# Left keys of two exponential tiles turned in one transpose, in an attention and MoE kernel

## The chip, the cores and the metric

The kernel runs on one core of a Trainium2 chip. The metric is the device time of one execution in microseconds; three runs of the kernel before gave 951.61 (median), 950.59 and 954.29. The engines are called PE (matrix products and transposes), DVE (vector), ACT (scalar, exponentials), POOL (GpSimd) and SP (issues the DMAs).

## The reference

```python
q_rot, k_rot = rotate(q), rotate(k)          # q, k, v: 4 x 8 heads x 576 x 64, f32
scores = 1/sqrt(64) * q_rot @ k_rot.T        # 576 x 576 for each of 32 heads
attn = exp(scores - max(scores, -1)); attn = attn / (sum(attn, -1) + 1e-9)
x = (attn @ v) -> 2304 x 512                 # heads side by side
x = (1/(1+exp(-(x @ w_gate))) * (x @ w_val)) @ w_out          # weights given in float64
h = x @ w_in; solu = h * softmax(h)
out = (solu - mean) / sqrt(var + 1e-6) * g_ln @ w_out2
```

## The kernel before

**Three stages.** Attention takes the first 290 us or so of the trace, then come the gated products (stage B) and the last layer (stage C). The change touches attention alone. There, work goes by 16 pairs of heads. A pair has 9 tiles of scores: four tiles of 128 queries for each head, and between them one tile (n = 4, `order[n] is None`) with the 64 left-over queries of both heads. 576 keys are 512 main keys and 64 left keys.

**One tile, step by step.** `scores` (L372) multiplies a tile of queries with the 576 keys, in two halves of 288 columns, into PSUM (tile `s`, two buffers). `row_max` (L379, tile `nm`) reduces it on DVE. `exps` (L384, tile `e`) takes exponentials on ACT. `transpose_e` (L442, tile `te`) turns the four 128-key blocks of `e` on PE, into one of three PSUM buffers of the pool `ps_t`. Each turned tile is then written twice: ACT writes the high part (`evac_h`, L433), and DVE the low part, which is the PSUM value less that high part (`evac_l`, L436). `attend` (L483, tile `av`) multiplies the result with v.

**Left keys.** `transpose_left` (L463, tile `tk`) runs twice for each pair, once for each head. It turns the last 64 columns of each of the head's four `e` tiles (64 partitions out, 128 columns in), into one PSUM tile of 64 x 512. ACT writes the high part to partitions 0 to 63 of `etl`, DVE the low part to partitions 64 to 127. `transpose_corner` (L454, tile `tl`) does so for the tile of left queries.

**Blocks of k and q.** For each pair `qk_bank` (L303, L306, tile `tq`) turns rotated k and q in three parts; ACT and DVE write them as blocks `st0` and `st1` (lines L433 and L436 again). `stack` copies blocks by DMA (L317 to L323), so that partitions 64 to 127 get what the low parts need. The first pair has no time for that and copies with ACT and DVE (`stack_first`, L332 to L338).

**What sets the order.** It is written out: an agenda gives each step a slot (`SLOTS`), nine slots to a pair, and one loop emits a slot: row maximum of the tile, the ACT copies, the exponentials, the DVE subtractions, then the scores of the next tile and the steps of the agenda. Each engine works off its own rows in that order. `left=(6, 11)` places the two `transpose_left` of a pair: head 0 in slot 6 of the pair, head 1 in slot 2 of the next. Weights for stage B are decoded on the side (`val`, `mag`, `w`), some operations to a pair from the fifth pair on.

Of the kernel before, what the change touches and what calls it, by code (L numbers as in the profile page):

```python
# [8 lines left out]
F32 = mybir.dt.float32  # L9
F32R = mybir.dt.float32r  # L10
# [10 lines left out]
def kernel(  # L21
# [21 lines left out]
    nc = tc.nc  # L43
    B, H, S, D = q.shape
# [3 lines left out]
    P = 128  # L48
    MAIN, LEFT, HALF = 512, 64, 288
# [14 lines left out]
    ident = const.tile([P, P], F32, name="ident")  # L64
# [112 lines left out]
    enter = a_ctx.enter_context  # L177
# [2 lines left out]
    rawv_p = prep_ctx.enter_context(tc.tile_pool(name="rawv", bufs=2, side="right"))  # L180
    rot_p = prep_ctx.enter_context(tc.tile_pool(name="rot", bufs=1, side="right"))
    qk_p = enter(tc.tile_pool(name="qkT", bufs=2))
    wt_p = enter(tc.tile_pool(name="wt", bufs=2))
    rt_p = enter(tc.tile_pool(name="rt", bufs=1))
    uw_p = enter(tc.tile_pool(name="uw", bufs=4))
    st_p = enter(tc.tile_pool(name="st", bufs=4))
    et_p = enter(tc.tile_pool(name="et", bufs=1))
    vs_p = enter(tc.tile_pool(name="vs", bufs=2))
    e_p = enter(tc.tile_pool(name="e", bufs=7))
    dr_p = enter(tc.tile_pool(name="dr", bufs=2, space=bass.MemoryType.DRAM))  # L190
    ps_2 = ctx.enter_context(tc.tile_pool(name="ps_2", bufs=2, space=PSUM, side="right"))
    ps_t = enter(tc.tile_pool(name="ps_t", bufs=3, space=PSUM))
# [4 lines left out]
    raws, stacks, vraws, vss = {}, {}, {}, {}  # L197
# [92 lines left out]

    def qk_bank(i, part):

        raw = turned[i].rearrange("p i h d -> p i (h d)")
        if part == 0:
            stacks[i, 0] = qk_p.tile([P, 2, 2, S], F32R, tag="st0", name=f"st0_{i}")
            stacks[i, 1] = qk_p.tile([P, 3, S], F32R, tag="st1", name=f"st1_{i}")
        st = stacks[i, 0]
        ps = ps_t.tile([P, 512], F32, tag="t", name=f"tq{i}_{part}")  # L300
        if part < 2:
            for r in range(4):
                nc.tensor.transpose(ps[:, r * P:(r + 1) * P], raw[:, 4 * part + r, :], ident)  # L303
            h_out, l_out, src = st[:, 0, part, 0:MAIN], st[:, 1, part, 0:MAIN], ps
        else:
            nc.tensor.transpose(ps[:, 0:P], raw[:, 8, :], ident)  # L306
            h_out, l_out = st[:, 0, :, MAIN:S], st[:, 1, :, MAIN:S]
            src = ps[:, 0:P].rearrange("p (a t) -> p a t", a=2)
        return [(h_out, l_out, src)]

    def stack(i, step):

        s0, s1 = stacks[i, 0].bitcast(F32), stacks[i, 1].bitcast(F32)
        flat = s0.rearrange("p a b s -> p (a b) s")
        dma = nc.sync.dma_start
        if step == 0:
            dma(out=s1[D:P, 0:2], in_=flat[D:P, 0:2])  # L317
            dma(out=s1[0:D, 2], in_=flat[D:P, 0])
            dma(out=s1[0:D, 0:2], in_=flat[D:P, 2:4])
            dma(out=s1[D:P, 2], in_=flat[D:P, 2])  # L320
        else:
            dma(out=flat[D:P, 0:2], in_=flat[0:D, 2:4])
            dma(out=flat[D:P, 2], in_=flat[0:D, 0])  # L323

    def stack_first(h, step):

        near, far = slice(h * D, (h + 1) * D), slice((1 - h) * D, (2 - h) * D)
        if step < 2:
            c = slice(0, MAIN) if step == 0 else slice(MAIN, S)
            srcs = [(first[kq] if step == 0 else first[2][:, kq])[near] for kq in range(2)]  # L330
            for kq, ps in enumerate(srcs):
                nc.scalar.copy(out=st_block(0, h, kq)[near, c], in_=ps)  # L332
            for kq, ps in enumerate(srcs):
                hi = st_block(0, h, kq)[near, c].bitcast(F32)
                nc.vector.tensor_sub(out=st_block(0, h, kq)[far, c], in0=ps, in1=hi)
        else:
            nc.scalar.copy(out=st_block(0, h, 2)[far], in_=st_block(0, h, 0)[near].bitcast(F32))
            nc.vector.tensor_copy(st_block(0, h, 2)[near], st_block(0, h, 0)[far].bitcast(F32))  # L338

    first = []  # L340

# [2 lines left out]
            (nc.gpsimd, nc.vector)[SLOTS["left_eng"]].tensor_copy(qtl[i % 2][:, 3 * h, :], st_block(i, h, 1)[:, MAIN:S].bitcast(F32))  # L344

    def st_block(i, h, j):
        t = stacks[i, h]
        return t[:, j // 2, j % 2, :] if h == 0 else t[:, j, :]


    order = [(0, 0), (0, 1), (0, 2), (0, 3), None, (1, 0), (1, 1), (1, 2), (1, 3)]
    NTL = len(order)
    e_tiles = {}
    sums = {}
    wts = {}
# [74 lines left out]
    etl = et_p.tile([P, 2, S], F32R, name="etl")  # L430
# [101 lines left out]
    def at(g, kind, fn, *args):  # L532
# [155 lines left out]
    if True:  # L688
# [154 lines left out]
    for t, (s, bl, f) in enumerate(items):  # L843
# [17 lines left out]
        if f % FG in (1, 2) and t + FG < len(items):  # L861
            s2, bl2, _ = items[t + FG]
# [4 lines left out]
    enter = c_ctx.enter_context  # L867
# [256 lines left out]
```

## Time and profile before

| | |
|---|---|
| runs, median (lowest, highest) | 951.61 us (950.59, 954.29) |
| profiled execution | 953.07 us, its span 951.2 us |
| attention, first to last row maximum | 14.7 to 286.4 us |
| PE busy over the span | 97% |
| DVE, ACT, POOL busy over the span | 67%, 52%, 47% |

The shares over the span are means over stages that have little in common; attention has to be read by itself. A row of the timeline gives the start, the length, engine, line, operation, what is written and read, the count, and in brackets the idle time before it and what ended that; an idle time that is too short to be told has no bracket and is read from the starts and lengths. Instructions of one engine overlap a little, so that a start can lie before the end of the one ahead. PE's matrix products overlap far more: the distance of their starts tells the pace. A row of the windows gives from:to, the length, the busy time with the count of instructions for PE, PE's weight loads, DVE, ACT and POOL, then the granted clock of PE, the DMA share and GB/s.

### The profile page before, as it was taken

The page shows a single profiled execution, that of the slowest core. Times are in us where ns is not written, and L with a number is a line of the kernel's source. Part 1 is how long each engine was busy: PE and PEld are TensorE (multiplying, and loading weights), DVE is VectorE, ACT ScalarE, POOL GpSimd, SP SyncE. Part 2 cuts the span into 40 slices and gives each one's busy share as a digit, 9 for nine tenths or more (in the row PEclk, how much of TensorE's full clock was granted, in tenths as well). Part 3 has the DMA queues.
Part 4 walks back from the last instruction along what each step waited for, and adds up shares of the span by engine and source line. Part 5 has one row for each costly group of instructions (what it writes and reads, how often), then busy time and mean ns, then how long its engine had stood idle before and what let it go on. Part 6 is the DMA issues. An engine that isn't in the chain of part 4 may idle for free.

```text
span 951.2 us, 14449 instructions
## 1 busy us (share of the span) xinstructions
PE 922.0 (97%) x5128; PEld 798.2 (84%) x5128; DVE 641.1 (67%) x1069; ACT 498.7 (52%) x994; POOL 447.1 (47%) x356
## 2 busy tenths in 40 slices
PE   4999999999998999999999999999999989999998
PEld 3999999999997688887888898788898778888886
DVE  6999999999998943446164456345366896666661
ACT  5999999998995322223111223011123676666662
POOL 7678899898935532335232344314344431121110
PEclk9999999999999999999999999999999999999999
DMA  4668676776644211022001013101012243344332
GB/s 121 156 159 195 172 191 165 187 179 161 142 128 143 89 45 45 23 65 91 1 22 45 23 45 102 32 23 39 28 46 89 88 78 78 67 83 83 67 78 45
DMA packets 92233, 86.12 MB, mean 91 GB/s; under 512 B 51568, under 2 KB 76416, under 8 KB 92160
## 3 DMA queue, kind: packets, MB, share of 16 engines
q1 hardware_dynamic: 92160, 85.19, 35.2%
q8 instruction: 41, 0.67, 0.3%
q14 instruction: 32, 0.26, 0.1%
HBM read 46.83 MB, written 4.79 MB: 54 GB/s over the span
## 4 chain that ended last, share of the span: by engine, by line
PE 82%; DVE 9%; POOL 2%; issue 2%; ACT 2%; DMA 2%; SPq 0%; DVEq 0%; POOLq 0%; ACTq 0%
PE gv L682 9%; PE gv L683 9%; PE gv L681 9%; PE s L372 8%; PE av L483 7%; PE te L442 5%; PE y L791 4%; PE y L789 4%; PE y L790 4%; PE po L977 3%; PE po L979 3%; PE po L978 3%; PE ph L882 3%; PE ph L884 3%; PE ph L883 3%
## 5 line engine op out<-in xcount | busy, mean ns | idle before, releaser
L775 POOL TENSOR_TENSOR gs<-g,gs 128x512 fp32r<-128x512 f32 (+1 forms) x59 | 74.1, 1255 | 261.3 <-DVE gs L774 211.3
L770 ACT ACTIVATE sg<-gv 128x512 f32<-128x512 f32 (+1 forms) x60 | 33.3, 555 | 287.8 <-PE gv L683 287.8
L681 PE MATMUL gv<-xs,w 128*128 128x512 f32 (+1 forms) x480 | 176.8, 368 | 2.5 <-ACT w L137 2.5
L683 PE MATMUL gv<-xs,w 128*128 128x512 f32 (+1 forms) x480 | 176.9, 369 | 1.8 <-POOL w L138 1.7
L682 PE MATMUL gv<-xs,w 128*128 128x512 f32 (+1 forms) x480 | 176.9, 368 | 1.0 <-DVE xs L516 1.0
L772 DVE TENSOR_TENSOR g<-gv,sg 128x512 f32<-128x512 f32 (+1 forms) x60 | 38.2, 636 | 174.6 <-ACT sg L770 165.0
L384 ACT ACTIVATE e<-s,nm 128x576 f32<-128x576 f32 x144 | 107.3, 745 | 11.6 <-DVE nm L379 11.2
L379 DVE TENSOR_REDUCE nm<-s 128x1 f32<-128x576 f32 x144 | 107.2, 745 | 4.6 <-PE s L372 3.0
L683 PEld LDWEIGHTS gv<-xs,w 128*128 128x128 f32 x480 | 90.5, 189 | 18.2 <-POOL w L138 2.8
L436 DVE TENSOR_TENSOR et<-te,et 128x512 fp32r<-128x512 f32 x144 | 98.2, 684 | 10.6 <-ACT et L433 10.1
L372 PE MATMUL s<-st 128*128 128x288 f32 x512 | 100.2, 318 | 5.2 <-ACT e L384 2.6
L681 PEld LDWEIGHTS gv<-xs,w 128*128 128x128 f32 x480 | 90.1, 188 | 17.8 <-ACT w L137 3.3
L682 PEld LDWEIGHTS gv<-xs,w 128*128 128x128 f32 x480 | 90.1, 188 | 17.4 <-DVE xs L516 2.8
L483 PE MATMUL av<-et,vs 128*128 128x288 f32 x512 | 100.0, 316 | 0.5 <-DVE uw L634 0.3
L791 PE MATMUL y<-gs,w 128*128 128x512 f32 (+1 forms) x240 | 88.4, 368 | 0.1
L790 PE MATMUL y<-gs,w 128*128 128x512 f32 (+1 forms) x240 | 88.2, 368 | 0.0
L789 PE MATMUL y<-gs,w 128*128 128x512 f32 (+1 forms) x240 | 88.2, 367 | 0.0
L442 PE MATMUL te<-ident,e 128*128 128x128 f32 x576 | 86.0, 272 | 0.0
L433 ACT CAST et<-te 128x512 fp32r<-128x512 f32 x144 | 83.8, 584 | 3.0 <-PE te L442 2.9
L372 PEld LDWEIGHTS s<-st 128*128 128x128 f32 x512 | 74.6, 193 | 12.3 <-ACT e L384 7.6
L483 PEld LDWEIGHTS av<-et,vs 128*128 128x128 f32 x512 | 73.0, 189 | 4.2 <-DVE uw L634 2.5
L442 PEld LDWEIGHTS te<-ident,e 128*128 128x128 f32 x576 | 70.4, 140 | 0.2
(125 smaller groups left out, 1955.0 us busy)
## 6 DMA issues: line engine op xcount, KB each, us to landing
st<-st SPq DMA_DIRECT2D x45, 288.0 KB
wraw<-in_moe_w_out_dram SPq DMA_DIRECT2D x20, 512.0 KB
st<-st SPq DMA_DIRECT2D x45, 144.0 KB
wraw<-in_moe_w_gate_dram SPq DMA_DIRECT2D x12, 512.0 KB
wraw<-in_moe_w_val_dram SPq DMA_DIRECT2D x12, 512.0 KB
um<-uw SPq DMA_DIRECT2D x32, 144.0 KB
rawv<-in_v_dram SPq DMA_DIRECT2D x16, 256.0 KB
wraw<-in_moe_w_in_dram SPq DMA_DIRECT2D x8, 512.0 KB
```

What stands on the lines that cost most here:

```text
L372: nc.tensor.matmul(ps[:, j, :HALF], w, x, start=m == 0, stop=m == len(mm) - 1)
L379: nc.vector.tensor_reduce(out=nm, in_=ps[:, :, :HALF], axis=AX.XY, op=ALU.max, negate=True)
L384: nc.scalar.activation(out=e.rearrange("p (j c) -> p j c", j=2), in_=ps[:, :, :HALF], func=AF.Exp, bias=nm, accum_out=sums[i][:, n:n + 1],)
L436: nc.vector.tensor_sub(out=l_out, in0=ps, in1=h_out.bitcast(F32))
L442: nc.tensor.transpose(ps[:, r * P:(r + 1) * P], e[:, r * P:(r + 1) * P], ident)
L483: nc.tensor.matmul(av[:, :HALF], *mm[m], start=m == 0, stop=m == len(mm) - 1)
L681: nc.tensor.matmul(ps[:, :n], wh, x[:, 0, :n], start=kk == 0, stop=False)
L682: nc.tensor.matmul(ps[:, :n], wh, x[:, 1, :n], start=False, stop=False)
L683: nc.tensor.matmul(ps[:, :n], wl, x[:, 0, :n], start=False, stop=kk == KD - 1)
L789: nc.tensor.matmul(ys[m][:, :n], wh, g[:, 0, :n], start=first, stop=False)
L790: nc.tensor.matmul(ys[m][:, :n], wl, g[:, 0, :n], start=False, stop=False)
L791: nc.tensor.matmul(ys[m][:, :n], wh, g[:, 1, :n], start=False, stop=last)
```

## The change

Left keys come to stand at the other end in every second tile. For that the blocks of k are made 640 columns long, with the left keys at both ends, and odd tiles take their scores from column 0, even tiles from column 64. Two tiles of exponentials share one buffer of 1152 columns, so the left keys of an even tile and of the odd one behind it are neighbours, and one transpose turns both: two transposes of 128 x 128 in place of four of 64 x 128. The result has an upper half (even tiles) and a lower half (odd tiles) and is written by two ACT and two DVE instructions in place of one of each. `qk_bank` gets a further small transpose in its third part and writes 192 columns there in place of 128. The first pair's copies of blocks go to ACT (head 0) and to two DMAs (head 1). Buffers: `wt`, `um` from 2 to 1, `uw` from 4 to 3, `e` from 7 to four doubles and one single.

```diff
-    wt_p = enter(tc.tile_pool(name="wt", bufs=2))
+    wt_p = enter(tc.tile_pool(name="wt", bufs=1))
-    uw_p = enter(tc.tile_pool(name="uw", bufs=4))
+    uw_p = enter(tc.tile_pool(name="uw", bufs=3))
-    e_p = enter(tc.tile_pool(name="e", bufs=7))
+    e_p = enter(tc.tile_pool(name="e", bufs=4))
+    el_p = enter(tc.tile_pool(name="el", bufs=1))
...
+    KW = LEFT + S
+    K_AT, Q_AT, K2_AT = 0, KW, KW + S
+    BLOCKS = ((K_AT, KW), (Q_AT, S), (K2_AT, KW))
     def qk_bank(i, part):
...
-            nc.tensor.transpose(ps[:, 0:P], raw[:, 8, :], ident)
-            h_out, l_out = st[:, 0, :, MAIN:S], st[:, 1, :, MAIN:S]
-            src = ps[:, 0:P].rearrange("p (a t) -> p a t", a=2)
+            nc.tensor.transpose(ps[:, LEFT:LEFT + P], raw[:, 8, :], ident)
+            nc.tensor.transpose(ps[:, 0:LEFT], raw[0:LEFT, 8, :], ident[0:LEFT, 0:LEFT])
+            h_out, l_out = (x.rearrange("p (b t) -> p b t", t=LEFT)[:, 0:19:9] for x in (h, l))
+            src = ps[:, 0:3 * LEFT].rearrange("p (a t) -> p a t", a=3)
...
     def stack_first(h, step):
...
-            nc.scalar.copy(out=st_block(0, h, 2)[far], in_=st_block(0, h, 0)[near].bitcast(F32))
-            nc.vector.tensor_copy(st_block(0, h, 2)[near], st_block(0, h, 0)[far].bitcast(F32))
+            if h == 0:
+                nc.scalar.copy(out=st_block(0, h, 2)[far], in_=st_block(0, h, 0)[near].bitcast(F32))
+                nc.scalar.copy(out=st_block(0, h, 2)[near], in_=st_block(0, h, 0)[far].bitcast(F32))
+            else:
+                nc.sync.dma_start(out=st_block(0, h, 2)[far].bitcast(F32), in_=st_block(0, h, 0)[near].bitcast(F32))
+                nc.sync.dma_start(out=st_block(0, h, 2)[near].bitcast(F32), in_=st_block(0, h, 0)[far].bitcast(F32))
...
-            c = slice(j * HALF, (j + 1) * HALF)
+            k0 = j * HALF + (0 if order[n] is not None and order[n][1] % 2 else LEFT)
+            c = slice(k0, k0 + HALF)
...
     def transpose_left(i, h):
         ps = ps_t.tile([P, 512], F32, tag="t", name=f"tk{i}_{h}")
-        n0 = 5 * h
-        for qt in range(4):
-            nc.tensor.transpose(ps[0:LEFT, qt * P:(qt + 1) * P], e_tiles.pop((i, n0 + qt))[:, MAIN:S], ident)
-        return [(etl[0:LEFT, h, 0:MAIN], etl[LEFT:P, h, 0:MAIN], ps[0:LEFT, :])]
+        for m in range(2):
+            nc.tensor.transpose(ps[:, m * P:(m + 1) * P], e_both.pop((h, m))[:, MAIN:MAIN + P], ident)
+        x = etl[:, h, 0:MAIN].rearrange("p (m a t) -> p a m t", m=2, a=2)
+        src = ps[:, 0:2 * P].rearrange("p (m t) -> p m t", m=2)
+        up, down = slice(0, LEFT), slice(LEFT, P)
+        return [(x[up, 0], x[down, 0], src[up]), (x[down, 1], x[up, 1], src[down])]
...
-        first_b=(-1, -1, 2),
+        first_b=(-1, -1, 0),
```

**DVE around the second `transpose_left` of pair 10** (slots 1 to 4 of pair 11; a name's first number is the pair, then the tile). Before:

```order
L436 TENSOR_TENSOR st0_12_3189<-tq12_2_3284,st0_12_3189 128x2x64
L397 RECIPROCAL sum10_2925<-sum10_2925 128x9
L379 TENSOR_REDUCE nm11_3_3325<-s11_3_3300 128x1
L436 TENSOR_TENSOR et_245<-te10_8_3305,et_245 128x4x128
L436 TENSOR_TENSOR etl_131<-tk10_1_3314,etl_131 64x512
L379 TENSOR_REDUCE nm11_4_3364<-s11_4_3333 128x1
```

and in the changed kernel:

```order
L468 TENSOR_TENSOR st0_12_3161<-tq12_2_3254,st0_12_3161 128x3x64
L429 RECIPROCAL sum10_2899<-sum10_2899 128x9
L405 TENSOR_REDUCE nm11_3_3294<-s11_3_3271 128x1
L468 TENSOR_TENSOR et_251<-te10_8_3276,et_251 128x4x128
L468 TENSOR_TENSOR etl_134<-tk10_1_3285,etl_134 64x2x128 x2
L405 TENSOR_REDUCE nm11_4_3334<-s11_4_3303 128x1
```

One subtraction of 64 x 512 became two of 64 x 256 ahead of the row maximum of tile 4, and the one of `st0` is 192 columns wide in place of 128. The order is the same.

**PE at the same place.** Before:

```order
L306 MATMUL tq12_2_3284<-ident_70,turned12_3078 128x128
L372 MATMUL s11_3_3300<-st0_11_2905 128x288 x4
L442 MATMUL te10_8_3305<-ident_70,e10_8_3201 128x128 x4
L483 MATMUL av10_10_3310<-et_245,vs10_2940 128x288 x2
L463 MATMUL tk10_1_3314<-ident_70,e10_5_3115 64x128
L463 MATMUL tk10_1_3314<-ident_70,e10_6_3147 64x128
L463 MATMUL tk10_1_3314<-ident_70,e10_7_3175 64x128
L463 MATMUL tk10_1_3314<-ident_70,e10_8_3201 64x128
L372 MATMUL s11_4_3333<-st0_11_2905,qtl1_79 128x288 x2
```

and in the changed kernel:

```order
L315 MATMUL tq12_2_3254<-ident_70,turned12_3051 128x128
L316 MATMUL tq12_2_3254<-ident_70,turned12_3051 128x64
L398 MATMUL s11_3_3271<-st0_11_2880 128x288 x4
L475 MATMUL te10_8_3276<-ident_70,e10_7_3146 128x128 x4
L518 MATMUL av10_10_3281<-et_251,vs10_2914 128x288 x2
L495 MATMUL tk10_1_3285<-ident_70,e10_5_3088 128x128
L495 MATMUL tk10_1_3285<-ident_70,e10_7_3146 128x128
L398 MATMUL s11_4_3303<-st0_11_2880,qtl1_79 128x288 x2
```

Two of the four transposes of left keys are gone, and a transpose of 64 columns stands behind the third part of k and q.

## Rows read from the trace of the kernel before

**Rows 1.** The page: the chain of waits that ended last, by engine.

```profile
PE 82%; DVE 9%; POOL 2%; issue 2%; ACT 2%; DMA 2%; SPq 0%; DVEq 0%; POOLq 0%; ACTq 0%
```

**Rows 2.** Windows of attention, pairs 1 to 2 and 10 to 11.

```profile
199.39:210.24 10.85, 10.85 (x86) 10.27 (x86) 10.66 (x19) 10.34 (x26) 9.98 (x10) 1.00 0.69 180
210.24:216.49 6.25, 6.25 (x50) 5.91 (x49) 5.91 (x9) 5.13 (x13) 6.09 (x4) 1.00 0.68 154
...
46.15:57.00 10.85, 10.85 (x86) 10.31 (x86) 10.66 (x19) 10.35 (x26) 6.79 (x6) 1.00 0.54 143
57.00:62.85 5.85, 5.85 (x49) 5.72 (x48) 4.98 (x9) 5.00 (x12) 5.62 (x5) 1.00 0.85 189
```

**Rows 3.** Timeline of DVE from pair 10's turned tile 4 on.

```profile
199.39 0.69 DVE L436 TENSOR_TENSOR et<-te,et 128x512 fp32r<-128x512 f32 x1 [0.33 <-ACT et L433]
200.11 0.68 DVE L436 TENSOR_TENSOR etl<-tk,etl 64x512 fp32r<-64x512 f32 x1
200.83 0.76 DVE L379 TENSOR_REDUCE nm<-s 128x1 f32<-128x576 f32 x1
201.50 0.68 DVE L436 TENSOR_TENSOR et<-te,et 128x512 fp32r<-128x512 f32 x1
```

**Rows 4.** Timelines of ACT and DVE, pair 11, tile 4 to turned tile 4.

```profile
211.09 0.74 ACT L384 ACTIVATE e<-s,nm 128x576 f32<-128x576 f32 x1 [0.28 <-DVE nm L379]
...
216.49 0.69 DVE L436 TENSOR_TENSOR et<-te,et 128x512 fp32r<-128x512 f32 x1 [0.17 <-ACT et L433]
```

**Rows 5.** Groups by form, all of the span: busy us, mean ns.

```profile
L436 DVE TENSOR_TENSOR etl<-tk,etl 64x512 fp32r<-64x512 f32 x32 | 21.9, 683 | 1.0
...
L433 ACT CAST etl<-tk 64x512 fp32r<-64x512 f32 x32 | 18.6, 582 | 0.6
...
L436 DVE TENSOR_TENSOR etl<-tl,etl 64x128 fp32r<-64x128 f32 x16 | 4.5, 283 | 0.5
...
L433 ACT CAST etl<-tl 64x128 fp32r<-64x128 f32 x16 | 4.2, 260 | 0.1
```

**Rows 6.** Timelines of PE and ACT around pair 10's second left keys.

```profile
208.02 0.63 PE L463 MATMUL tk<-ident,e 128*64 128x128 f32 x4
208.44 1.31 PE L372 MATMUL s<-st,qtl 128*128 128x288 f32 x8
...
208.10 0.19 ACT L384 ACTIVATION_READ_ACCUMULATOR e<-s,nm 128x1 f32 x1
```

**Rows 7.** Timelines of the first pair: DVE; ACT; PE and SP towards the second pair.

```profile
11.85 1.23 DVE L338 CAST st<-st 64x576 fp32r<-64x576 f32 x1
13.11 1.58 DVE L335 TENSOR_TENSOR st<-tq,st 64x512 fp32r<-64x512 f32 x4
...
21.08 0.89 DVE L436 TENSOR_TENSOR st<-tq,st 128x512 fp32r<-128x512 f32 x2 [0.16 <-ACT st L433]
...
23.26 0.76 DVE L379 TENSOR_REDUCE nm<-s 128x1 f32<-128x576 f32 x1
...
11.08 0.67 ACT L337 CAST st<-st 64x576 fp32r<-64x576 f32 x1
11.77 1.29 ACT L332 CAST st<-tq 64x512 fp32r<-64x512 f32 x4
...
31.08 0.78 PE L372 MATMUL s<-st 128*128 128x288 f32 x4
...
27.66 0.46 SPq L323 DMA_DIRECT2D st<-st  x1
```

**Rows 8.** Timelines: weight loads and SP, fourth pair's scores; POOL and SP, pair 11.

```profile
65.04 0.43 PEld L372 LDWEIGHTS s<-st 128*128 128x128 f32 x3 [0.34 <-DMA st<-st]
...
61.96 0.46 SPq L323 DMA_DIRECT2D st<-st  x1
...
215.76 1.43 POOL L495 TENSOR_TENSOR x_sb<-uw,um 64x576 f32<-64x576 f32 x1
...
218.59 0.51 SPq L489 DMA_DIRECT2D um<-uw  x1
```

More of the change, by code (lines that the diff above doesn't have):

```diff
@@ L296, in qk_bank @@
         if part == 0:
-            stacks[i, 0] = qk_p.tile([P, 2, 2, S], F32R, tag="st0", name=f"st0_{i}")
-            stacks[i, 1] = qk_p.tile([P, 3, S], F32R, tag="st1", name=f"st1_{i}")
+            stacks[i, 0] = qk_p.tile([P, 2 * (KW + S)], F32R, tag="st0", name=f"st0_{i}")
+            stacks[i, 1] = qk_p.tile([P, 2 * KW + S], F32R, tag="st1", name=f"st1_{i}")
         st = stacks[i, 0]
+        h, l = st[:, 0:KW + S], st[:, KW + S:]
         ps = ps_t.tile([P, 512], F32, tag="t", name=f"tq{i}_{part}")
@@ L303, in qk_bank @@
                 nc.tensor.transpose(ps[:, r * P:(r + 1) * P], raw[:, 4 * part + r, :], ident)
-            h_out, l_out, src = st[:, 0, part, 0:MAIN], st[:, 1, part, 0:MAIN], ps
-        else:
-            nc.tensor.transpose(ps[:, 0:P], raw[:, 8, :], ident)
-            h_out, l_out = st[:, 0, :, MAIN:S], st[:, 1, :, MAIN:S]
-            src = ps[:, 0:P].rearrange("p (a t) -> p a t", a=2)
+            c = slice((LEFT, Q_AT)[part], (LEFT, Q_AT)[part] + MAIN)
+            h_out, l_out, src = h[:, c], l[:, c], ps
+        else:
+            nc.tensor.transpose(ps[:, LEFT:LEFT + P], raw[:, 8, :], ident)
+            nc.tensor.transpose(ps[:, 0:LEFT], raw[0:LEFT, 8, :], ident[0:LEFT, 0:LEFT])
+            h_out, l_out = (x.rearrange("p (b t) -> p b t", t=LEFT)[:, 0:19:9] for x in (h, l))
+            src = ps[:, 0:3 * LEFT].rearrange("p (a t) -> p a t", a=3)
         return [(h_out, l_out, src)]
@@ L313, in stack @@
         s0, s1 = stacks[i, 0].bitcast(F32), stacks[i, 1].bitcast(F32)
-        flat = s0.rearrange("p a b s -> p (a b) s")
         dma = nc.sync.dma_start
+        kq, both, k2 = slice(0, KW + S), slice(KW + S, 2 * (KW + S)), slice(K2_AT, K2_AT + KW)
         if step == 0:
[L317 to L320, printed above, removed]
-        else:
-            dma(out=flat[D:P, 0:2], in_=flat[0:D, 2:4])
-            dma(out=flat[D:P, 2], in_=flat[0:D, 0])
+            dma(out=s1[D:P, kq], in_=s0[D:P, kq])
+            dma(out=s1[0:D, k2], in_=s0[D:P, 0:KW])
+            dma(out=s1[0:D, kq], in_=s0[D:P, both])
+            dma(out=s1[D:P, k2], in_=s0[D:P, k2])
+        else:
+            dma(out=s0[D:P, kq], in_=s0[0:D, both])
+            dma(out=s0[D:P, k2], in_=s0[0:D, 0:KW])
@@ L325, in stack_first, with block @@
     def stack_first(h, step):
         near, far = slice(h * D, (h + 1) * D), slice((1 - h) * D, (2 - h) * D)
+        parts = []
         if step < 2:
[L329 to L335, printed above, removed]
-        else:
-            nc.scalar.copy(out=st_block(0, h, 2)[far], in_=st_block(0, h, 0)[near].bitcast(F32))
-            nc.vector.tensor_copy(st_block(0, h, 2)[near], st_block(0, h, 0)[far].bitcast(F32))
+            for kq in range(2):
+                if step == 0:
+                    places, ps = slice((LEFT, 0)[kq], (LEFT, 0)[kq] + MAIN), first[kq][near]
+                else:
+                    places, ps = slice(0, 10, 9) if kq == 0 else slice(8, 9), first[2][near, 2 * kq:2 + kq]
+                parts.append((kq, places, ps))
+            def block(kq, places, rows):
+                x = st_block(0, h, kq)
+                return x[rows, places] if step == 0 else x.rearrange("p (b t) -> p b t", t=LEFT)[rows, places]
+            for kq, places, ps in parts:
+                nc.scalar.copy(out=block(kq, places, near), in_=ps)
+            for kq, places, ps in parts:
+                hi = block(kq, places, near).bitcast(F32)
+                nc.vector.tensor_sub(out=block(kq, places, far), in0=ps, in1=hi)
+        else:
+            if h == 0:
+                nc.scalar.copy(out=st_block(0, h, 2)[far], in_=st_block(0, h, 0)[near].bitcast(F32))
+                nc.scalar.copy(out=st_block(0, h, 2)[near], in_=st_block(0, h, 0)[far].bitcast(F32))
+            else:
+                nc.sync.dma_start(out=st_block(0, h, 2)[far].bitcast(F32), in_=st_block(0, h, 0)[near].bitcast(F32))
+                nc.sync.dma_start(out=st_block(0, h, 2)[near].bitcast(F32), in_=st_block(0, h, 0)[far].bitcast(F32))
@@ L346, in st_block @@
     def st_block(i, h, j):
-        t = stacks[i, h]
-        return t[:, j // 2, j % 2, :] if h == 0 else t[:, j, :]
+        at, n = BLOCKS[j]
+        return stacks[i, h][:, at:at + n]
     order = [(0, 0), (0, 1), (0, 2), (0, 3), None, (1, 0), (1, 1), (1, 2), (1, 3)]
     NTL = len(order)
-    e_tiles = {}
+    e_tiles, e_both = {}, {}
     sums = {}
@@ L382, in exps @@
     def exps(i, n, ps, nm):
-        e = e_p.tile([P, S], F32, tag="e", name=f"e{i}_{n}")
+        if order[n] is None:
+            e = el_p.tile([P, S], F32, tag="el", name=f"el{i}")
+        else:
+            h, qt = order[n]
+            if qt % 2 == 0:
+                e_both[h, qt // 2] = e_p.tile([P, 2 * S], F32, tag="e", name=f"e{i}_{n}")
+            e = e_both[h, qt // 2][:, qt % 2 * S:(qt % 2 + 1) * S]
         nc.scalar.activation(
@@ L440, in transpose_e @@
         ps = ps_t.tile([P, 512], F32, tag="t", name=f"te{i}_{n}")
+        k0 = LEFT if order[n] is not None and order[n][1] % 2 else 0
         for r in range(4):
-            nc.tensor.transpose(ps[:, r * P:(r + 1) * P], e[:, r * P:(r + 1) * P], ident)
+            nc.tensor.transpose(ps[:, r * P:(r + 1) * P], e[:, k0 + r * P:k0 + (r + 1) * P], ident)
         if order[n] is not None:
```

## The prediction

> **What bounds the kernel now.** I read four views in this order. First the chain of waits by engine [rows 1]: PE holds 82% of it, DVE 9%. Taken at its word, fewer transposes mean less time. But it is one chain over three stages, so attention needs its own views. Second, the windows of two pairs of attention [rows 2]. I cut each pair at two points of DVE: where it subtracts the turned tile 4, and where it ends the row maximum of tile 4 of the next pair. The stretch from the first to the second, which I call the long stretch, lasts 10.85 us in pairs 10 to 11 and 10.85 us in pairs 1 to 2, with 10.66 us of DVE work in 19 instructions in both, although POOL and the DMAs do quite different amounts in the two. A length that stays equal while other engines' work changes, and that is filled to 0.19 us by one engine, is that engine's sum. The 0.19 left is about 0.01 for each instruction. So DVE sets the long stretch. The other stretch, back to the next turned tile 4, lasts 5.85 us where no weights are decoded and 6.25 us where some are; DVE works 4.98 and 5.91 us there and waits a little for ACT, as ACT does for DVE [rows 4]: a short circle of row maximum, exponential, copy and subtraction. A period is thus 16.7 to 17.1 us.
>
> Third, where the change falls. Both subtractions of left keys (tile `tk`) of a pair lie in long stretches: one right behind the turned tile 4's successor, one in the middle of the first rows shown [rows 3]. The subtraction of the third part of k and q lies there too. Fourth, what PE waits for beside them [rows 6]: four `tk` transposes start at 208.02, and the scores behind them at 208.44, 0.42 us later. The exponential whose end frees their PSUM tile reads out at 208.10 + 0.19 = 208.29. PE is therefore only 0.15 us behind what it would wait for anyway, and shorter transposes let it wait for ACT, which waits for DVE. So PE's busy 10.85 us of 10.85 [rows 2] is not its need: the ends of matrix products are modelled, and a busy PE is not a PE at its pace.
>
> **What the change costs, part by part.**
>
> *Left keys on DVE.* Before: one subtraction of 64 x 512, 0.683 us [rows 5]. After: two of 64 x 256. That shape is not in the trace; between 64 x 128 (0.283) and 64 x 512 (0.683) a column costs 1.04 ns, so 256 columns take 0.283 + 0.133 = 0.416. The gap between instructions counts as well. An ordinary pair of neighbours overlaps: the row maximum at 200.83 would end at 201.59, and the next subtraction starts at 201.50, 0.09 sooner. Around the subtraction of left keys there is no overlap: the one ahead ends at 200.08, it starts at 200.11; it ends at 200.79, the row maximum starts at 200.83 [rows 3]. This instruction reads partitions 0 to 63 and writes 64 to 127, unlike its neighbours. The startup agrees: a copy that shifts partitions ends at 13.08 and the next subtraction starts at 13.11 [rows 7]. In the change the first half shifts down and the second shifts up, so they differ from each other as well. If the second is held too, the place takes 0.03 + 0.416 + 0.03 + 0.416 + 0.04 = 0.93 in place of 0.03 + 0.683 + 0.04 = 0.75: **+0.18 us for each `tk`**. If the second overlaps the first by 0.09, it is +0.06. Less than that would need the pair to cost less than its columns; nothing in the rows allows a gain. I take +0.18, since every partition shift shown was held.
>
> [...]
>
> *Third part of k and q.* The subtraction grows from 128 to 192 columns, 64 x 1.04 ns = +0.07, in each long stretch. DVE's sum there: 2 x 0.18 + 0.07 = **+0.43 us**.
>
> *The same on ACT.* One `tk` copy of 0.582 us [rows 5] becomes two. A column costs (582 - 260) / 384 = 0.84 ns, so 256 columns take 0.367, and a pair costs 0.05 more if the copies overlap as ordinary ones do by about 0.10. Held ones cost more: the shifting copy at 11.08 ends at 11.75 and the next starts at 11.77 [rows 7], so held on both sides the added half costs 0.15 + 0.15 = 0.30. The third part adds 64 columns, 0.05. ACT is busy 10.34 us of the long stretch's 10.85 [rows 2], and starts the next exponential 0.28 us after going idle [rows 4]; I count 0.03 for a copy that comes late for DVE, and keep 0 and 0.35 a pair as ends.
>
> *PE.* Each `tk` loses two transposes: their pace is 0.42 / 4 = 0.105 us [rows 6], so 0.21 us twice a pair. The third part gains one of 64 columns, at most 0.105. A net 0.3 us a pair leaves PE, beside DVE's stretch, so I count nothing; PE's wait for the exponential grows instead. If PE were the limit, this is worth its full size (a rival below).
>
> *Startup.* DVE loses its copy at 11.85, which is hidden since PE waits for POOL's rotated k after it, and the second one, ahead of the row maximum of tile 3: subtractions end at 21.08 + 0.89 = 21.97, the row maximum starts at 23.26 [rows 7], so 1.29 us is the most that can go. ACT gets one more copy of about 0.67 early, in time it has to spare. The two new DMAs of the first pair are issued in its first slot and wanted five tiles later; a block copy needs 65.04 - 61.96 = 3.08 us from issue to use [rows 8]. The same sum bounds the gain: the second pair's scores cannot start before 27.66 + 3.08 = 30.74, and start at 31.08 now [rows 7], so 0.34 is the least if the issue doesn't move forward. I take -0.9, as the issue follows DVE and moves too.
>
> *Buffers and DMAs.* One buffer less each for `wt`, `um`, `uw`: the tightest is `um`, whose next DMA is issued at 218.59, 1.40 us after POOL's last read ends at 215.76 + 1.43 = 217.19 [rows 8]. It holds, so nothing is added. Were it short, SP would wait with the block copies queued behind it and the next pair's scores behind those. Block DMAs get 5 to 11% longer, which matters only where scores wait for them, 0.34 us at pair 3 [rows 8]. That wait also swallows about 0.3 of what DVE loses ahead of it, as it is not DVE's.
>
> *Sum.* 14 long stretches from a pair to the next carry both `tk` and the third part: 14 x 0.43 = 6.0. The last, into pair 15, carries no third part: +0.36. ACT's late copies, 14 x 0.03 = 0.4. Less 0.3 at pair 3 and 0.9 at the startup: **+5.6, some 5.4 with a little of it lost in the circle's slack**. The profiled execution of 953.07 us (span 951.2 and 1.9 around it) would become 958.5. It stood 1.46 above the median of the runs, 951.61; on that scale the forecast is **957.0 us**. Its own range is 955.3 to 958.7: the gain at the startup between 0.34 and 1.29, 0 to 0.07 a pair at ACT, 0.40 to 0.46 at DVE.
>
> **The rivals.**
>
> *The second half is not held.* Each `tk` costs +0.06, the third part +0.07, 0.19 a stretch: 14 x 0.19 + 0.12 - 0.3 - 0.9 = +1.6, **953.2 us**. For it: no row shows opposite shifts in a row. Against it: every shift that rows show waited for its neighbour on both sides.
>
> *PE is the limit after all.* Then 0.42 - 0.105 = 0.31 us a pair goes, 14.5 x 0.31 = 4.5, with 0.9 from the startup -5.4: **946.2 us**; with half of that gain lost to DVE, 949. For it: the chain [rows 1] and PE busy through both stretches. Against it: the long stretch is DVE's sum to 0.19 us [rows 2], and the scores behind `tk` come only 0.15 us after their exponential. It decides if DVE's added work finds idle time of more than 0.43 us a stretch; the rows show less than half of that.
>
> *ACT becomes the bound.* It has 10.85 - 10.34 = 0.51 us to spare in a long stretch. Held copies of opposite shifts take 2 x 0.30 + 0.05 = 0.65. If that goes on the circle in full, since DVE's subtraction needs ACT's copy, the sum is 14 x 0.65 + 0.6 - 0.9 = +8.8: **960.4 us**. For it: the held copy at 11.08. Against it: DVE has the longer row, and ACT works ahead of it at the `tk` copy, so most of it lies beside DVE's own 0.43.
>
> **How the numbers follow.** Forecast 0.58, second half not held 0.18, PE the limit 0.12, ACT the bound 0.10, and 0.02 for a short buffer. A measurement of this kernel can tell about 0.5% from no change: 946.85 and 956.37. Of the forecast's own range some seven tenths lie above 956.37: 0.42, with ACT's and the buffer's 0.11 that is 0.53 slower. PE as the limit gives 0.07 faster and the rest within. That leaves 0.40 for no change. The range from 951.8 to 960.0 takes in the rival without holding and leaves out PE's and a part of ACT's.
>
> **What would show it.** Right: in all pairs the long stretch is 11.2 to 11.3 us in place of 10.85, still filled by DVE, with 20 or 21 instructions; the other stays at 5.8 to 6.3; the second half of a `tk` subtraction starts about 0.03 us after the first one's end; a half takes 0.40 to 0.43; scores behind `tk` wait longer for an exponential; tile 3's row maximum of the first pair comes about 1 us sooner. Wrong: the second half starts before the first ends (first rival); the long stretch is shorter than 10.85 (PE's rival); DVE has gaps of 0.2 us and more there that end with ACT's copies (ACT's rival); or SP waits ahead of `um`'s DMA.

## The result, and the profile after

The changed kernel is slower: 960.78 us (median of five runs, 960.50 to 963.21) beside 951.90 (950.59 to 954.29), a ratio of 1.0094 with a 95% interval of 1.0081 to 1.0108. In a later set of runs it gave 960.91 beside 952.91, 1.0086 (1.0072 to 1.0100). The direction was forecast; the size was not. 957.0 us was +5.4, measured were +8.9 and +8.0, and 960.78 lies above the range's upper end of 960.0.

The page's chain after the change (PE 81%, DVE 7%, ACT 4%) reads much as before [rows 1] and says nothing of the loss. The windows do. These are the two stretches of [rows 2], cut at the same instructions of DVE: pairs 10 to 11, then 1 to 2, each with the stretch that follows.

```profile
205.79:217.35 11.56, 11.43 (x85) 10.28 (x84) 11.25 (x22) 10.92 (x28) 9.35 (x9) 1.00 0.60 150
217.35:223.20 5.85, 5.85 (x47) 5.59 (x46) 5.51 (x9) 4.90 (x13) 5.69 (x4) 1.00 0.69 158
47.47:59.02 11.55, 11.42 (x86) 10.29 (x84) 11.25 (x21) 10.91 (x28) 7.37 (x6) 1.00 0.66 165
59.02:64.88 5.86, 5.86 (x47) 5.56 (x46) 5.07 (x9) 4.91 (x13) 5.62 (x5) 1.00 0.80 179
```

The long stretch went from 10.85 to 11.55 us, again the same in early and late pairs: **+0.70 where 0.43 was forecast**. DVE's busy time rose from 10.66 to 11.25, by 0.59, so DVE also waits 0.1 more than it did. Its timeline, from the turned tile 4 of pair 10 (compare [rows 3]) to the second `tk`, shows where:

```profile
205.79 0.69 DVE L468 TENSOR_TENSOR et<-te,et 128x512 fp32r<-128x512 f32 x1
206.52 0.86 DVE L468 TENSOR_TENSOR etl<-tk,etl 64x256 fp32r<-64x256 f32 x2
207.41 0.76 DVE L405 TENSOR_REDUCE nm<-s 128x1 f32<-128x576 f32 x1
208.19 0.69 DVE L468 TENSOR_TENSOR et<-te,et 128x512 fp32r<-128x512 f32 x1
...
214.59 0.35 DVE L468 TENSOR_TENSOR st<-tq,st 128x192 fp32r<-128x192 f32 x1
...
214.97 0.70 DVE L405 TENSOR_REDUCE nm<-s 128x1 f32<-128x576 f32 x1
215.74 0.69 DVE L468 TENSOR_TENSOR et<-te,et 128x512 fp32r<-128x512 f32 x1
216.46 0.86 DVE L468 TENSOR_TENSOR etl<-tk,etl 64x256 fp32r<-64x256 f32 x2
217.35 0.76 DVE L405 TENSOR_REDUCE nm<-s 128x1 f32<-128x576 f32 x1
```

The kernel before, third part of k and q to the turned tile 8:

```profile
207.89 0.28 DVE L436 TENSOR_TENSOR st<-tq,st 128x128 fp32r<-128x128 f32 x1
...
208.21 0.70 DVE L379 TENSOR_REDUCE nm<-s 128x1 f32<-128x576 f32 x1
208.82 0.68 DVE L436 TENSOR_TENSOR et<-te,et 128x512 fp32r<-128x512 f32 x1
```

Five places make up the 0.70. From the end of the turned tile (206.48) to the row maximum (207.41) it takes 0.93 in place of 0.75, +0.18, and as much at the second `tk`: as forecast, term by term. The third part of k and q takes 0.35 in place of 0.28: +0.07, as forecast. But from the row maximum at 207.41 to the subtraction at 208.19 it is 0.78, and was 0.67 between the same two in [rows 3]: +0.11. And from the row maximum at 214.97 to the next subtraction it is 0.77, and was 0.61 in the kernel before (208.21 to 208.82): +0.15. These last two were not in the sum, and they differ: at the first, ACT's copy of that tile had ended at 207.74, long before; at the second it ends at 215.70, and DVE starts 0.04 behind it.

Over all of attention, measured on the two profiled executions of the changed kernel (963.21 us, the slowest of its five runs, and 960.52) against the one of before (953.07):

| | forecast | first profile | second |
|---|---|---|---|
| start to row maximum of pair 0, tile 4 | -0.9 | +0.36 | -0.92 |
| the 15 long stretches | +6.5 | +9.70 | +9.66 |
| the 15 stretches between | 0 | -1.33 | -1.57 |
| all that follows | 0 | +1.41 | +0.28 |
| sum | +5.6 | +10.14 | +7.45 |

The row "all that follows" is what is left of the difference in device time. In it the granted clock differs too: it fell from 1.00 to 0.50 for 6.8 us at 318.4 and at 772.4 in the first profile, for 3.4 us at 318.5 and at 772.5 in the second, and for 3.4 us at 765.4 in the kernel before. Ahead of 318.4 in the first profile, PE was busy for 15.7 of 18.4 us, ahead of 772.4 for 5.4 of 7.4. How much of that row this makes is not shown.

### The profile page after: what moved, and what is told of

Its sections match the earlier page's. It is cut to its first block, busy times and chain, and to the rows that moved or that the text cites. A ratio compares the mean times of both kernels' runs of the same rounds, so it can differ in the third digit from the quotient of the medians.

```text
span 961.4 us, 14529 instructions
## 1 busy us (share of the span) xinstructions
PE 932.2 (97%) x5080; PEld 800.2 (83%) x5080; DVE 647.2 (67%) x1099; ACT 505.9 (53%) x1026; POOL 447.1 (47%) x356
## 4 chain that ended last, share of the span: by engine, by line
PE 81%; DVE 7%; ACT 4%; issue 3%; POOL 2%; DMA 2%; SPq 0%; ACTq 0%; DVEq 0%; POOLq 0%
PE gv L717 9%; PE gv L718 9%; PE gv L716 9%; PE s L398 8%; PE av L518 7%; PE te L475 5%; PE y L824 4%; PE y L825 4%; PE y L826 4%; PE po L1013 3%; PE po L1012 3%; PE po L1014 3%; PE ph L917 3%; PE ph L918 3%; PE ph L919 3%
## 5 line engine op out<-in xcount | busy, mean ns | idle before, releaser
L416 ACT ACTIVATE e<-s,nm 128x576 f32<-128x576 f32 x128 | 95.6, 747 | 5.3 <-DVE nm L405 4.4
L475 PE MATMUL te<-ident,e 128*128 128x128 f32 x512 | 77.3, 275 | 0.0
L475 PEld LDWEIGHTS te<-ident,e 128*128 128x128 f32 x512 | 63.3, 141 | 0.2
```

The lines of the kernel that those rows point to most:

```text
L416: nc.scalar.activation(out=e.rearrange("p (j c) -> p j c", j=2), in_=ps[:, :, :HALF], func=AF.Exp, bias=nm, accum_out=sums[i][:, n:n + 1],)
L475: nc.tensor.transpose(ps[:, r * P:(r + 1) * P], e[:, k0 + r * P:k0 + (r + 1) * P], ident)
```

## The experiments

Theory D is DVE with its held instructions, those that start only after the one ahead has ended (0.03 us behind it at `tk` in [rows 3], where the row maximum and the subtraction behind it overlap by 0.09); the rivals are ACT, PE, and the rest of the change. A window below is always the long stretch from pair 10's turned tile 4, as above.

**Is PE's saved work worth anything?** The kernel before, with two of the four turns, each read twice by ACT and DVE:

```diff
-            nc.tensor.transpose(ps[0:LEFT, qt * P:(qt + 1) * P], e_tiles.pop((i, n0 + qt))[:, MAIN:S], ident)
...
+            if qt > 1:
+                nc.tensor.transpose(ps[0:LEFT, (qt - 2) * P:(qt - 1) * P], e[:, MAIN:S], ident)
+        src = ps[0:LEFT, 0:2 * P].unsqueeze(1).to_broadcast([LEFT, 2, 2 * P])
...
```

> The kernel before with two of the four tk transposes left out; ACT and DVE read the two turned blocks twice, in instructions of the same size, so two tiles in four get the left keys of others. Theory D (DVE sets the long stretch): 10.85 as before, scores behind tk wait longer for an exponential, time 951.4 to 952.4. Rival (PE sets it): 0.21 less at each of two places in 15 pairs, 6.3 us, time about 945.6.

951.46 us beside 952.45, ratio 0.9987 (0.9978 to 0.9996): about a microsecond, not six. The stretch did not move by 0.01:

```profile
198.17:209.02 10.85, 10.79 (x83) 9.93 (x82) 10.66 (x19) 10.19 (x26) 10.03 (x10) 1.00 0.77 186
```

PE is 0.06 less busy there, and DVE's 10.66 is the same to the digit. The rival of PE has fallen: what the change saves on PE lies beside DVE.

**Two instructions, or two opposite shifts?** The kernel before, with each `tk` written in two halves that both shift down:

```diff
-        return [(etl[0:LEFT, h, 0:MAIN], etl[LEFT:P, h, 0:MAIN], ps[0:LEFT, :])]
+        halves = (slice(0, 2 * P), slice(2 * P, 4 * P))
+        return [(etl[0:LEFT, h, c], etl[LEFT:P, h, c], ps[0:LEFT, c]) for c in halves]
```

> The kernel before with its ACT copy and its DVE subtraction of each tk cut into two of 64 x 256, both shifting the same way as now; nothing else. Theory D (opposite partitions are what holds the second half): the second half overlaps the first by 0.08, a tk place takes 0.78 in place of 0.716, the row maximum and the subtraction behind are as before: long stretch 10.85 + 2 x 0.06 = 10.97, time 953.2 to 954.2. Rival (two instructions cost as much wherever they lie): 0.89 and 0.115 at each, long stretch 11.3 or more, time 957 or more.

954.41 us beside 952.84, ratio 1.0018 (1.0009 to 1.0027). DVE's timeline and the window:

```profile
199.95 0.69 DVE L436 TENSOR_TENSOR et<-te,et 128x512 fp32r<-128x512 f32 x1 [0.45 <-ACT et L433]
200.67 0.75 DVE L436 TENSOR_TENSOR etl<-tk,etl 64x256 fp32r<-64x256 f32 x2
201.45 0.76 DVE L379 TENSOR_REDUCE nm<-s 128x1 f32<-128x576 f32 x1
202.12 0.68 DVE L436 TENSOR_TENSOR et<-te,et 128x512 fp32r<-128x512 f32 x1
```

```profile
199.95:210.93 10.98, 10.97 (x86) 10.27 (x86) 10.79 (x22) 10.41 (x28) 9.93 (x10) 1.00 0.69 176
```

The two halves take 0.75 together, 0.86 in the changed kernel with the same shapes. The stretch grows by 0.13 and not by 0.70, and the subtraction behind the row maximum (201.45 to 202.12, 0.67) is not late. Splitting is a fifth of the loss; that the sides are opposite costs 0.12 more at each `tk`, and with the 0.11 behind the row maximum that is 0.35 of the 0.70.

**Why is the subtraction late behind the row maximum?** The changed kernel, halves in the other order, so that the half that DVE subtracts last before the row maximum is read from partitions 0 to 63 in place of 64 to 127:

```diff
-        return [(x[up, 0], x[down, 0], src[up]), (x[down, 1], x[up, 1], src[down])]
+        return [(x[down, 1], x[up, 1], src[down]), (x[up, 0], x[down, 0], src[up])]
```

> The changed kernel with the two halves of each tk written in the other order on ACT and DVE: lower half of PSUM first, upper half last. [...] On ACT the exponential behind overlaps the last half (0.13 sooner). Long stretch 11.55 -> 11.44 by DVE's place alone, to 11.3 if the late copy of turned tile 8 goes too; time 957.3 to 959.2. Rival (the gap behind the row maximum has another cause, ACT or PE): gap stays, long stretch 11.55, time 960.3 to 961.3.

DVE, then ACT at the same `tk`, then the window, and last ACT at that place in the changed kernel:

```profile
204.73 0.69 DVE L468 TENSOR_TENSOR et<-te,et 128x512 fp32r<-128x512 f32 x1
205.51 0.86 DVE L468 TENSOR_TENSOR etl<-tk,etl 64x256 fp32r<-64x256 f32 x2
206.40 0.76 DVE L405 TENSOR_REDUCE nm<-s 128x1 f32<-128x576 f32 x1
207.07 0.68 DVE L468 TENSOR_TENSOR et<-te,et 128x512 fp32r<-128x512 f32 x1
```

```profile
204.12 0.58 ACT L465 CAST et<-te 128x512 fp32r<-128x512 f32 x1
204.72 0.76 ACT L465 CAST etl<-tk 64x256 fp32r<-64x256 f32 x2
```

```profile
204.73:216.27 11.54, 11.40 (x86) 10.34 (x85) 11.14 (x22) 10.98 (x28) 9.29 (x9) 1.00 0.58 148
```

```profile
205.65 0.76 ACT L465 CAST etl<-tk 64x256 fp32r<-64x256 f32 x2
206.43 0.74 ACT L416 ACTIVATE e<-s,nm 128x576 f32<-128x576 f32 x1
```

That the order of the halves makes the subtraction late is shown: from the row maximum to it is 0.67 again, for 0.78. DVE is busy 0.11 less. But the time is not: 960.51 us, ratio 1.0079 (1.0067 to 1.0091), stretch 11.54. ACT's first half now starts 0.02 behind the copy ahead of it, where the upper half had overlapped it (205.18 + 0.58 and 205.65 in the changed kernel: 0.11 sooner). So ACT's second half ends only at 204.72 + 0.76 = 205.48, and DVE's first half starts 0.03 behind that end: 205.51 - 205.42 = 0.09 behind its neighbour in place of 0.04, 0.05 later, at both `tk`. It reads only the first copy, which had ended about 0.4 us sooner, so its wait seems to cover both. One held start was exchanged for a wait; this experiment misses as to time, and shows what the 0.11 goes with.

**Is it ACT?** One ACT copy of 128 x 256 in place of the two halves:

```diff
...
-        return [(x[up, 0], x[down, 0], src[up]), (x[down, 1], x[up, 1], src[down])]
+        return [(x[:, 0], None, src), (x[up, 0], x[down, 1], src[up], True), (x[down, 0], x[up, 1], src[down], True)]
```

(`None`: ACT only; `True`: DVE only.)

> The changed kernel with one ACT copy of 128 x 256 for each tk in place of two of 64 x 256; DVE keeps two subtractions with opposite shifts. The high parts of odd tiles stand in the wrong half of a column block, so the left keys' share of the result is not that of the reference. ACT's row from the copy's start to the exponential's falls from 0.785 to about 0.27 us. Rival (ACT carries the loss): the long stretch falls from 11.55 to 11.1 or less, time about 954 to 956. Theory D (DVE carries it, ACT only the late copy of turned tile 8, 0.146): long stretch 11.40, both tk places unchanged on DVE (0.89 and 0.115 behind the row maximum), time 958.5 to 959.3.

```profile
203.53 0.39 ACT L466 CAST etl<-tk 128x256 fp32r<-128x256 f32 x1
203.80 0.77 ACT L416 ACTIVATE e<-s,nm 128x576 f32<-128x576 f32 x1
```

```profile
203.68:215.24 11.56, 11.25 (x86) 10.30 (x85) 11.25 (x22) 10.17 (x26) 9.37 (x9) 1.00 0.62 155
```

ACT's place fell from 0.78 to 0.27 us and its busy time by 0.75, and the stretch did not move: 961.75 us, ratio 1.0091 (1.0078 to 1.0104). The rival of ACT had the right number, 960.4, by accident. The 0.15 at the turned tile 8, which I had laid to ACT's halves, is not theirs either.

**Then whose is it?** In the changed kernel PE reaches the scores of the next tile late at the third part of k and q, and ACT's copy of it starts behind that:

```profile
213.37 0.27 PE L315 MATMUL tq<-ident,turned 128*128 128x128 f32 x1
213.57 0.27 PE L316 MATMUL tq<-ident,turned 64*128 64x64 f32 x1
213.77 0.81 PE L398 MATMUL s<-st 128*128 128x288 f32 x4
```

```profile
213.88 0.32 ACT L465 CAST st<-tq 128x192 fp32r<-128x192 f32 x1 [0.16 <-PE tq L316]
```

The edit turns 128 rows where 64 were turned, a larger transpose of which half is overwritten:

```diff
+            nc.tensor.transpose(ps[:, 0:P], raw[:, 8, :], ident)
             nc.tensor.transpose(ps[:, LEFT:LEFT + P], raw[:, 8, :], ident)
-            nc.tensor.transpose(ps[:, 0:LEFT], raw[0:LEFT, 8, :], ident[0:LEFT, 0:LEFT])
```

> The changed kernel with the second transpose of k's and q's third part turned from 128 x 128 like the first, written first and overlapped by it, in place of the 64 x 64 one; same values. Theory: the 64 x 64 one holds up PE on both sides (0.40 us from the 128 x 128 one to the scores where rows of 128 columns follow each other at 0.11), so ACT's copy, the exponential and the copy of turned tile 8 come late, and DVE waits 0.06 behind the row maximum where it overlapped by 0.08 before. Then: transpose to scores 0.22 us, that wait gone, long stretch 11.55 -> 11.41, time 958.3 to 959.3. Rival (the wider ACT copy of the third part alone makes it late): the wait stays, long stretch 11.55, time 960.3 or more.

```profile
212.17 0.27 PE L315 MATMUL tq<-ident,turned 128*128 128x128 f32 x1
212.28 0.27 PE L316 MATMUL tq<-ident,turned 128*128 128x128 f32 x1
212.31 0.78 PE L398 MATMUL s<-st 128*128 128x288 f32 x4
```

```profile
204.61:216.06 11.45, 11.25 (x85) 10.24 (x84) 11.20 (x21) 10.92 (x28) 9.23 (x9) 1.00 0.63 156
```

From the first transpose to the scores it is 0.14 us, and was 0.40 with the smaller one (0.03 in the kernel before, where the scores follow the first transpose directly: 206.64 and 206.67), so 64 rows of 64 columns cost more here than 128 of 128. The loss lies in two steps of 0.20, from the transpose ahead to that one and from it to the scores; no run shows what in 64 rows causes it. Fewer columns alone do not cost this: behind `tl`, with 128 rows and 64 columns, the scores of the kernel before start 0.03 later (202.78 and 202.81). The stretch is 0.10 shorter, of 0.15. The other 0.05 stay, 0.66 from the row maximum to the subtraction for 0.61; ACT's wider copy of the third part (0.32 for 0.27) would fit, as the rival had it. In time, 960.07 us, ratio 1.0078 (1.0065 to 1.0090), this is 1.4 us by the stretches and not to be told from the changed kernel's interval.

**The halves against all the rest.** The changed kernel with the left keys turned and written as before, blocks and buffers as now:

```diff
-        for m in range(2):
-            nc.tensor.transpose(ps[:, m * P:(m + 1) * P], e_both.pop((h, m))[:, MAIN:MAIN + P], ident)
+        for qt in range(4):
+            left = slice(0, LEFT) if qt % 2 else slice(MAIN, S)
+            nc.tensor.transpose(ps[0:LEFT, qt * P:(qt + 1) * P], e_tiles.pop((i, 5 * h + qt))[:, left], ident)
...
+        return [(etl[0:LEFT, h, 0:MAIN], etl[LEFT:P, h, 0:MAIN], ps[0:LEFT, :])]
```

> The changed kernel with the left keys of a head turned by four transposes of 64 x 128 into a PSUM tile of 64 x 512 and written by one ACT copy and one DVE subtraction, as before; the blocks of 640 columns, the pairs of exponentials, the 64 x 64 transpose, the wider third part and the buffers stay. If the writing of the halves is what costs, the long stretch falls to 10.85 + 0.07 (third part) + about 0.12 (64 x 64 transpose) = 11.0 to 11.05, time about 954 to 955.5. Rival (the blocks, DMAs or buffers carry the loss): long stretch 11.3 or more, 957 or more.

```profile
203.06:214.13 11.07, 11.01 (x85) 10.18 (x84) 10.82 (x19) 10.34 (x25) 9.06 (x9) 1.00 0.63 155
```

956.47 us beside the changed kernel's 960.91 on the same chip, ratios to before of 1.0038 (1.0025 to 1.0051) and 1.0086. The stretch is 11.07, 0.22 over before: 0.07 for the third part and 0.15 in the wait behind it, of which the 128-row transpose above gave back 0.10. So two thirds of the 0.70 is the writing of the halves (2 x 0.18 and 0.11), one third the blocks with left keys at both ends. In time the halves are 4.4 of the 8.0 us; the time is 1 us above what I expected.

> The changed kernel once more, beside the two above. Long stretch 11.55 in each pair again; time 960 to 961.5. The first pair tells whether its startup of the first profile (row maximum of tile 4 ends 0.36 us later than before) comes again, or stands 0.5 to 1.5 us earlier as in the kernels made from it.

It came again: 11.55, and the startup stood 0.92 earlier than before, not 0.36 later.

**What are the larger transposes worth if writing costs little?** One ACT copy and one DVE subtraction of 128 x 256, without a shift (`return [(x[:, 0], x[:, 1], src)]`):

> The changed kernel with one ACT copy of 128 x 256 and one DVE subtraction of 128 x 256 for each tk, without a shift of partitions; low parts stand beside high parts in the wrong half, so the left keys' share of the result is not that of the reference. It tells what the transposes are worth where writing them out costs little. Theory D: a tk costs DVE 0.33 in place of 0.89 + 0.115, the long stretch falls to 10.85 - 2 x 0.38 + 0.07 = 10.15 as long as DVE sets it, time about 943. Rival (PE is close behind): PE's own 10.85 less 0.3 = 10.55 is then the stretch, time about 948 to 949.

```profile
197.41:207.70 10.29, 10.23 (x81) 9.64 (x80) 10.13 (x20) 9.85 (x25) 9.87 (x10) 1.00 0.74 186
207.70:214.14 6.44, 6.44 (x52) 6.16 (x51) 5.82 (x9) 5.16 (x13) 6.28 (x4) 1.00 0.78 174
```

949.5 us, ratio 0.9966 (0.9953 to 0.9980), and not 943. The long stretch came out at 10.29 for 10.15, with DVE filling it. But the stretch behind it became longer than before (6.44 for 6.25). At its start DVE waits 0.35 us for ACT's copy, which waits for PE:

```profile
208.15 0.59 ACT L465 CAST et<-te 128x512 fp32r<-128x512 f32 x1 [0.50 <-PE te L475]
```

In the kernel before that wait of ACT was 0.23, and DVE had none. So where DVE no longer sets the pace, PE seems to, in the other stretch; that PE is busy throughout it says nothing, as it was so before (6.25 of 6.25). Three microseconds are what was had, and only with left keys that need no shift; I know of no layout that does so.

**Two repairs.** The changed kernel with the halves swapped and with the 128-row transpose, both as above:

> The changed kernel with two edits: the full-row transpose of the third part and the halves of tk written lower half first. Their gains in the long stretch were 0.10 and 0.02 alone. If they add up, the stretch is 11.43, time about 959; if the lower half's late ACT copy now ends last in both places, 11.45 to 11.55, 960.

They add up: 11.44 us, 959.58 us, ratio 1.0070 (1.0056 to 1.0083). The last idea was to set the corner's subtraction (`tl`), which shifts the same way, beside that of `tk`. In the kernel before:

> The kernel before with the corner's transpose (tile tl) in slot 6 of a pair, ahead of the first tk, in place of slot 8. Both subtractions shift the same way, so they stand side by side. Theory D: one held start and one held row maximum fewer, 0.23 a long stretch (10.85 -> 10.62), time 948.3 to 949.5. Rival (PE's three PSUM buffers of turned tiles, all taken in one slot, make PE wait): no gain or a loss, 952 to 955.

```profile
200.68 0.28 DVE L436 TENSOR_TENSOR etl<-tl,etl 64x128 fp32r<-64x128 f32 x1
200.89 0.67 DVE L436 TENSOR_TENSOR etl<-tk,etl 64x512 fp32r<-64x512 f32 x1
...
205.75 0.68 DVE L436 TENSOR_TENSOR et<-te,et 128x512 fp32r<-128x512 f32 x1
206.52 0.69 DVE L436 TENSOR_TENSOR st<-tq,st 128x512 fp32r<-128x512 f32 x1
```

The two subtractions do overlap, but DVE now waits for ACT's copies at two other places: at the second part of k and q (0.09 where it overlapped by 0.08), and behind the row maximum at 208.71, from where it is 0.72 to the next subtraction for 0.61 before. The stretch is 10.91, and the kernel is slower, as the rival had it: 954.86, ratio 1.0018 (1.0009 to 1.0027). In the changed kernel, with the other two edits:

> The changed kernel with three edits: the full-row transpose of the third part, the halves of tk written lower half first, and the corner's transpose in slot 6 behind the tk so that its subtraction follows the upper half's without a change of partitions. Theory D: 0.146 less from the transpose, 0.115 less behind each row maximum but 0.06 more ahead of each first half, 0.23 less from the corner: long stretch 11.55 -> 11.1 to 11.2, time 954.5 to 956. Rival (PSUM buffers or ACT become the wait): 957 to 960.

962.22, ratio 1.0099 (1.0086 to 1.0113): the rival again, and worse, with a stretch of 11.66. Its trace shows PE waiting twice for DVE's subtractions, 0.33 and 0.38 us, which fits the PSUM buffers of turned tiles; the second:

```profile
206.49 0.63 PE L310 MATMUL tq<-ident,turned 128*128 128x128 f32 x4 [0.38 <-DVE etl L468]
```

Behind that ACT's copies come late for DVE at five places of the stretch, 0.05 to 0.24 us each. No version here that computes all of the reference is faster than the kernel before.

## Why the prediction was wrong

**What bounds the kernel: right.** DVE sets the long stretch; half the turns left out changed it by nothing, and ACT's place at `tk` cut to a third changed it by nothing. Some readings on the way were off without touching the sum. The long stretch is cut where the row maximum of tile 4 starts, not where it ends. Its 0.19 us without DVE work is not 0.01 for each instruction but six gaps of 0.03, on both sides of the three subtractions that shift (two `tk`, one `tl`); the rest overlap. The first `tk` stands right behind the turned tile 4, the second right behind the turned tile 8, at 209.53. And the ends named for the range give 955.8 to 958.5, a little less than was stated.

**Left keys on DVE: right to 0.01, but it stopped too early.** Halves and price were those forecast (0.18 at each place; the gap between the halves was 0.01, not 0.03), and the case without opposite shifts is excluded. The step that failed is the end of its sum, "the place takes 0.03 + 0.416 + 0.03 + 0.416 + 0.04": I closed the account at the row maximum and let the subtraction behind it overlap as before. It is late as well, +0.11 in each long stretch (the second such place lies in the other stretch, which has room for it). It goes with the half that DVE subtracts last ahead of the row maximum: read from partitions 64 to 127, the subtraction behind the row maximum starts 0.78 after it; read from 0 to 63, it is 0.67, in the run with the halves swapped and in the one with both halves shifting down. Why that reaches past a row maximum is not shown by a run.

**ACT and PE: the second miss.** "I count 0.03 for a copy that comes late for DVE" was the right place with the wrong cause and a fifth of the size: 0.15. And of the transpose of 64 columns, "at most 0.105" for PE, was no bound: from rows of whole 128-row transposes I took the price of one that is not. It took 0.26 more than a full one, and PE, counted as nothing because it lies "beside DVE's stretch", stood there at the head of the chain PE, ACT, DVE; the 128-row transpose gave back 0.10 of the 0.15. Of a stretch 0.43 and 0.03 for ACT were forecast, 0.46; the two misses add 0.11 and 0.12 and make it 0.69 of the 0.70 measured. Over 14 stretches that is 3.2 us of the 3.8 by which 960.78 lies above 957.0; the startup and the other stretch go against each other in the first profile.

**Startup: right, with more scatter than I gave it.** Tile 3's row maximum came 1.08 us sooner in the first profile and 1.35 in the second, as forecast; tile 4's was then +0.36 and -0.92, and the cause of that is under what I had not expected. In the nine traces with the new startup, tile 4's row maximum ends between 24.33 and 26.24 us, with 25.19 in the middle; in the four with the old one, between 25.75 and 25.90. So -0.7 is the middle where I had -0.9.

**The other stretch: -1.3 to -1.6, which I had at nothing.** I had taken the 6.25 us of decoding pairs as a circle that does not change; it holds an instruction whose length goes with what POOL runs beside it (L123, 1.15 us at 213.24 in the kernel before and 0.67 at 220.35 in the changed one).

## What to carry to other kernels

Where an engine runs back to back, price an edit by the gaps around it as well as by its columns (here 0.03 us on both sides of a subtraction that shifts, where the next pair overlaps by 0.09), and look past the next instruction: here the subtraction behind the row maximum came 0.11 later too. Do not count on a transpose of fewer rows to be cheaper because it has fewer columns (here one of 64 x 64 held the scores back 0.26 us longer than one of 128 x 128): look for a row of that shape, or give it a bound that allows for a wait on both sides. And undo one half of a change alone before believing a rival whose sum fits.

## What the runs showed that I had not expected

**DVE's decoding seems to wait for POOL.** The kernel before, pair 11, DVE and POOL; then the changed kernel, pair 11 and pair 10:

```profile
213.24 1.15 DVE L123 SCALAR_TENSOR_TENSOR val<-mag,val 128x512 int32<-128x512 int32 x1
```

```profile
212.41 3.27 POOL L253 TENSOR_TENSOR turned<-raw,other 128x576 f32<-128x576 f32 x2
```

```profile
202.57 1.18 DVE L122 TENSOR_SCALAR val<-wraw 128x512 int32<-128x512 int32 x1
...
220.35 0.67 DVE L123 SCALAR_TENSOR_TENSOR val<-mag,val 128x512 int32<-128x512 int32 x1
```

```profile
200.67 2.80 POOL L254 TENSOR_TENSOR turned<-raw,other 128x576 f32<-128x576 f32 x2
...
218.91 3.40 POOL L254 TENSOR_TENSOR turned<-raw,other 128x576 f32<-128x576 f32 x2
```

Each POOL row holds two instructions. The one running when L123 starts at 213.24 ends at 213.84; L123 ends 0.55 later, and did so after each of the six of its kind in the kernel before. L122 ends 0.28 or 0.29 after POOL's where it starts well inside one. In the changed kernel L123 happens to start as POOL's instruction ends and takes 0.67, while POOL's next one takes 2.02 in place of 1.89; but L122 now starts in the middle of one in pairs 7 and 10, 1.13 and 1.18 us for 0.40. So six pairs got 0.4 shorter and two 0.5 longer, from nothing but a shift of when they start. That is most of the -1.3 to -1.6. That POOL is the cause is read from these rows; no run here changed the phase by itself.

**PE's slower level in the first pair.** PE starts again at 18.41 us in the first profile, after 0.41 us of idling, and at 18.30 in the second, after 0.40. From there to the transposes below it is busy without a break, and the first transposes follow each other at 0.22 us in both. The eight transposes of tiles 0 and 1, first profile, then second:

```profile
21.94 1.91 PE L475 MATMUL te<-ident,e 128*128 128x128 f32 x8
```

```profile
21.71 1.04 PE L475 MATMUL te<-ident,e 128*128 128x128 f32 x8
```

They follow each other at 0.21 us in the one and at half of that in the other. Later in the first profile, products of 128 x 512 follow each other at 0.43 us where the granted clock reads 0.50 (320.17 to 324.86) and at 0.23 where it reads 1.00 (325.51 to 331.87), so the slower transposes look like the lower clock. The windows read a granted clock of 1.00 for both, but the trace's record of that clock begins only at 24.9 us in the first profile and at 21.6 in the second, and what lies ahead of it is counted as 1.00; the pace of the transposes doubles at about these times. Of the nine traces with the new startup, the two in which the record begins last (24.2 and 24.9 us) are those with the latest row maximum (25.87 and 26.24). That is most of the 1.28 us between +0.36 and -0.92: the same kernel, the same work, another moment at which PE came up to speed.
